# A linear-attention and mixture-of-experts kernel: the state's decay and its copy on VectorE instead of GpSimd

## The chip, the cores and the metric

The kernel runs on one core of a Trainium2 chip. A core has five engines with an instruction stream each: TensorE (PE) multiplies matrices, VectorE (DVE) and GpSimd (POOL) do elementwise work, ScalarE (ACT) copies and applies functions, and SyncE (SP) issues most DMAs. Each takes its own instructions in order; between engines they wait for semaphores. The metric is the device time of one execution in microseconds (us), the median of several runs.

## What is computed

A recurrent attention layer (4 batches, 8 heads, 768 steps, head dimension 40) and behind it a mixture of 8 experts with a normalised gate (3072 tokens of 320 numbers, 1024 hidden):

```python
for t in range(S):
    y[:, :, t] = np.einsum('bhd,bhde->bhe', rt, state)
    Sa = np.einsum('bhde,bhe->bhd', state, at)
    state_decay = state * wt[:, :, None, :] - np.einsum('bhd,bhe->bhde', Sa, bt)
    state = state_decay + np.einsum('bhd,bhe->bhde', vt, kt)
```

```python
logits = x @ w_gate                   # x is y, a row of 320 per token
P = np.exp(logits - logits.max())
for _ in range(8):
    P /= P.sum(1, keepdims=True) + 1e-09
    P /= P.sum(0, keepdims=True) + 1e-09
    P *= N / E
for e in range(E):
    out += P[:, e:e + 1] * (np.maximum(x @ w1[e], 0.0) @ w2[e])
```

Everything is float32.

## The kernel before

**Attention** works in 12 chunks of 64 steps. A step of the kernel is one chunk of one batch, with its 8 heads as 4 pairs (rows 0 to 39 hold one head of a pair, rows 64 to 103 the other); there are 48 such steps. Each has two parts.

`prep(c, b)` (lines 106 to 165) does what does not depend on the state. It loads `inp`, takes running products of the decay along the chunk (`q` at L114, `g` at L122, both scans on DVE), scales keys (`kb`, L133) and the `a` vectors (`ab`, L139 and L140) with them, multiplies the two on PE (`ll`, L145), and transposes `kb` (`kt`, L153). The last column of `q`, the decay over the whole chunk, four numbers per row, is copied into `cc` at L138, since `q` has one buffer and is soon overwritten. `kb` is POOL's in all steps but the first, `ab` from the seventh step on (`NFAST` = 6); before that they are DVE's. For some steps the tiles `cc`, `g`, `sx`, `bb`, `kb` or `inp` lie inside larger raw tiles named `st`, and the trace then shows `st` in their place.

Between the parts stands a block inversion, once per two chunks (`GROUPS`, 6 in all): L170 to L182 on DVE, products of two tensors (`pr`) and reductions, up to 2048 numbers per row, ended by a copy at L331. Its results go to DRAM and back and are put together by PE and ACT (`tload`, `tmat`).

`recur(c, b)` (lines 235 to 302) is the chain through the state: on PE `av` (L251), `xc` (L259), `pu` (L270) and `c2` (L277, `c` in the trace), with the masks `f` (L252) and `pm` (L272) and the sum `ws` (L279) on DVE, and copies on ACT. From `ws` POOL makes the output `y` (L281), and the last 40 columns, the state before decay, are multiplied by the next chunk's `cc` to give `z` (L292). PE transposes `z` (`zt`, L297), ACT copies it into `vz` and `f`, and the next chunk of that batch starts from there. For chunks 0 to 8 `z` is POOL's, for 9 and 10 DVE's; chunk 11 has none.

The four batches run a little apart. Events with times (`ev`, lines 346 to 382) give the order in which the code is written, with up to 17 prepared steps in store (`NSX`). The framework's scheduler then makes each engine's order from its own estimate of when things are ready, so an edit to one instruction can move others.

**The experts** come next (`layer1`, `layer2`). Their first weights and inputs are transformed while attention ends (`prep_w` on POOL and ACT; `prep_x` on DVE and ACT, L517 to L533). From the ninth of 128 blocks on the order is written out by hand (`manual_schedule`); before that it is the scheduler's.

Of the kernel before, what the change touches and what calls it, by code (L numbers as in the profile page):

```python
# [28 lines left out]
def attention(ctx, tc, d, xd, ps, pq, pt, gs, lg):  # L29
    nc = tc.nc  # L30
# [59 lines left out]
    def first_use(i):  # L90
        if i in fresh:
            fresh.discard(i)
            nc.gpsimd.memset(bb_b[i], 0.0)
            nc.scalar.copy(out=sx_b[i][64:R2].rearrange("r p h x -> r (p h) x")[:, :, 64:104],
                           in_=cst[64:R2, 360:400].unsqueeze(1).broadcast_to([40, 8, 40]))
# [3 lines left out]
    def rot(key, lst):  # L99
        i = state[key]  # L100
        state[key] = (i + 1) % len(lst)
        return lst[i]
# [3 lines left out]
    def prep(c, b, ld):  # L106
        cb = c * NB + b
        inp = raws[IN_MAP[cb]][0:R2, 0:1284] if IN_MAP.get(cb) else pin.tile([R2, 1284], F32, name="inp", bufs=2)
        nc.sync.dma_start(out=inp, in_=d["inp"][c, b])
        w65 = inp[:, 0:516]  # L110
        kb_in = inp[:, 516:1028].rearrange("r (p k t) -> r p k t", p=NP, k=2)
        a_in = inp[:, 1028:1284].rearrange("r (p t) -> r p t", p=NP)
        q = pin.tile([R2, NP, 65], F32, name="q")
        nc.vector.tensor_tensor_scan(  # L114
            out=q.rearrange("r p t -> r (p t)"), data0=w65[:, 0:260], data1=one65,
            initial=0.0, op0=ALU.mult, op1=ALU.add)
        g1 = rot("g1", g1_b)
        nc.vector.reciprocal(out=g1[:, :, 0], in_=q[:, :, 64])
        sx = rot("sx", sx_b)
        i = next(j for j in range(NSX) if sx_b[j] is sx)  # L120
        g, bb, cc = g_b[i], bb_b[i], cc_b[i]
        nc.vector.tensor_tensor_scan(  # L122
            out=g.rearrange("r p t -> r (p t)"), data0=w65[:, 260:516],
            data1=g1.rearrange("r p t -> r (p t)"), initial=0.0, op0=ALU.mult, op1=ALU.add)
        if cb < NKB:
            raw = raws[KB_SETS[cb % len(KB_SETS)]]
            kb = raw[0:R2, 0:512].rearrange("r (p k t) -> r p k t", p=NP, k=2)
            lt = raw[0:64, 512:1024].rearrange("r (p k t) -> r p k t", p=NP, k=2)
        else:
            kb = pin.tile([R2, NP, 2, 64], F32, name="kb")  # L130
            lt = pin.tile([64, NP, 2, 64], F32, name="lt")
        eng = nc.vector if cb < NFAST else nc.gpsimd
        (nc.gpsimd if cb in KB_POOL else eng).tensor_tensor(  # L133
            out=kb, in0=kb_in,
            in1=q[:, :, 63::-1].unsqueeze(2).broadcast_to([R2, NP, 2, 64]), op=ALU.mult)
        ab = rot("ab", ab_b)
        first_use(i)
        nc.gpsimd.tensor_copy(out=cc, in_=q[:, :, 64])  # L138
        eng.tensor_tensor(out=ab[0:40, :, 0:64], in0=a_in[0:40], in1=g[0:40], op=ALU.mult)  # L139
        eng.tensor_tensor(out=ab[64:104, :, 64:128], in0=a_in[64:104], in1=g[64:104], op=ALU.mult)  # L140
        nc.scalar.copy(out=sx[64:104, :, 0, 0:64], in_=ab[0:40, :, 0:64])
        nc.scalar.copy(out=sx[64:104, :, 1, 0:64], in_=ab[64:104, :, 64:128])
        ll = pq.tile([128, NP, 2, 64], F32, name="ll", tag="pq")
        for p in range(NP):
            nc.tensor.matmul(ll[:, p], lhsT=kb[:, p], rhs=ab[:, p], start=True, stop=True)  # L145
        if cb < NKB:
            nc.scalar.activation(out=lt, in_=ll[64:128], func=AF.Copy, scale=-1.0)
            (nc.sync if cb < N_SP else nc.scalar).dma_start(out=ld[GRP[c][1], :, b], in_=lt)
            kt = pt.tile([128, NP, 2, 64], F32, name="kt", tag="pt")
        else:  # L150
            kt = pq.tile([128, NP, 2, 64], F32, name="kt", tag="pq")
        for p in range(NP):
            nc.tensor.transpose(kt[:, p].rearrange("s h x -> s (h x)")[:, 0:R2],  # L153
                                kb[:, p].rearrange("r k s -> r (k s)"), ident[0:R2, 0:R2])
        nc.vector.tensor_tensor(
            out=sx[0:64, :, :, 0:64], in0=ll[0:64],
            in1=mask_u.unsqueeze(1).unsqueeze(1).broadcast_to([64, NP, 2, 64]), op=ALU.mult)
        if cb >= NKB:
            nc.scalar.activation(out=lt, in_=ll[64:128], func=AF.Copy, scale=-1.0)
        nc.scalar.copy(out=sx[0:64, :, :, 64:104], in_=kt[0:64, :, :, 0:40])  # L160
        nc.scalar.activation(out=bb[0:64, :, 0:40], in_=kt[64:128, :, 0, 0:40], func=AF.Copy, scale=-1.0)
        nc.scalar.activation(out=bb[64:128, :, 64:104], in_=kt[64:128, :, 1, 0:40], func=AF.Copy, scale=-1.0)
        if cb >= NKB:
            (nc.sync if cb < N_SP else nc.scalar).dma_start(out=ld[GRP[c][1], :, b], in_=lt)
        return dict(cc=cc, g=g, sx=sx, bb=bb)
# [69 lines left out]
    def recur(c, b):  # L235
# [7 lines left out]
                          in_=d["vt"][c, b].rearrange("s (g x) -> s g x", x=40))  # L243
# [6 lines left out]
        for p in range(NP):  # L250
            nc.tensor.matmul(av[:, p], lhsT=vz[:, p], rhs=rb[:, p], start=True, stop=True)  # L251
        nc.vector.tensor_tensor(  # L252
            out=f[:, :, :, 0:64], in0=av,
# [24 lines left out]
        ws = wk.tile([R2, NP, 104], F32, name="ws")  # L278
# [5 lines left out]
        for h in range(2):  # L284
            nc.sync.dma_start(
                out=xd[h * 160:h * 160 + 160].rearrange("(p e) t -> e p t", e=40)[:, :, tok:tok + 64],
                in_=y[h * 64:h * 64 + 40])
        gq.append(gate(c, b, y))
        if c + 1 == NCH:
            return  # L290
        z = wk.tile([R2, NP, 40], F32, name="z", bufs=4)
        (nc.vector if c >= 9 else nc.gpsimd).tensor_tensor(out=z, in0=ws[:, :, 64:104],  # L292
                                in1=preps[c + 1, b]["cc"].unsqueeze(2).broadcast_to([R2, NP, 40]), op=ALU.mult)
        yield
        zt = ps.tile([40, NP, 104], F32, name="zt", tag="ps")
# [52 lines left out]
    def step(c, b):  # L348
        if (c, b) not in gens:
            gens[c, b] = recur(c, b)  # L350
        next(gens[c, b], None)

    def do_prep(s, c, b, first):
        if first:
            start_seg(s)
        preps[c, b] = prep(c, b, invs[s][0])
# [453 lines left out]
```

## Time and profile before

| | us |
|---|---|
| median of 3 runs (lowest, highest) | 1890.27 (1883.09, 1900.79) |
| the profiled execution | 1888.5 |
| its span, first to last instruction | 1886.7 |
| PE busy in the span | 1768.5 |
| DVE busy | 1395.1 |
| POOL busy | 896.9 |
| ACT busy | 853.9 |
| mean granted TensorE clock | 0.945 of full speed |

The span is what the profile's times count in; the rest of the execution's time lies around it. [...] In the lines of the profile `out<-in` gives the tiles that an instruction writes and reads, and `[1.28 <-POOL z L292]` says that the engine sat idle for 1.28 us before it, until the named instruction was done. `un`, `lu`, `pr` and `gt` are the tiles of the inversion.

### The profile page before, as it was taken

How to read it: one execution, taken by the hardware profiler on the slowest of the kernel's cores; microseconds unless marked ns; L12 is line 12 of the kernel's file. 1: busy time of each engine (PE TensorE's matmuls, PEld its weight loads, DVE VectorE, ACT ScalarE, POOL GpSimd, SP SyncE). 2: the span in 40 equal slices, each digit the busy share in tenths (PEclk: the TensorE clock that was granted, in tenths of full speed). 3: DMA queues.
4: the chain of work that ended last, by engine and by line, in shares of the span. 5: the costliest groups of instructions: out<-in, count | busy, mean ns of one | idle time of the engine just before them, and what ended most of it. 6: DMA issues, size and time to landing. Idle time of an engine off the chain costs nothing.

```text
span 1886.7 us, 31821 instructions
## 1 busy us (share of the span) xinstructions
PE 1768.5 (94%) x12035; PEld 1731.1 (92%) x12035; DVE 1395.1 (74%) x2330; ACT 853.9 (45%) x1845; POOL 896.9 (48%) x845
## 2 busy tenths in 40 slices
PE   4478989889998999999999999999999999999999
PEld 4368878789888999999999999999999999999999
DVE  7766768686579877776867777886776767777676
ACT  6346566655553444343433434345343433434342
POOL 6636457562345355371835628004461826537170
PEclk9568889988889999999999999999999999999999
DMA  8567777855732011110201102111110201111011
GB/s 192 102 131 160 137 156 144 176 128 102 164 96 70 32 43 37 37 61 14 73 26 49 55 19 74 55 33 38 37 55 19 73 19 56 37 37 57 17 37 42
DMA packets 187838, 136.26 MB, mean 72 GB/s; under 512 B 155941, under 2 KB 165285, under 8 KB 187685
## 3 DMA queue, kind: packets, MB, share of 16 engines
q1 hardware_dynamic: 184485, 128.98, 27.6%
q10 hardware_dynamic: 3200, 5.25, 1.1%
q8 instruction: 95, 1.56, 0.3%
q14 instruction: 58, 0.48, 0.1%
HBM read 113.74 MB, written 20.45 MB: 71 GB/s over the span
## 4 chain that ended last, share of the span: by engine, by line
PE 76%; DVE 10%; DMA 6%; issue 3%; POOL 2%; ACT 2%; SPq 1%; DVEq 0%; POOLq 0%; ACTq 0%
PE op L610 35%; PE p L545 32%; DMA inp<-in_inp_dram 2%; PE xc L259 2%; DVE pr L179 2%; PE pu L270 1%; PE av L251 1%; PE c L277 1%; DVE q L114 1%; PE ll L145 1%; PE lp L307 1%; PE gp L226 1%; DMA nd<-pr 1%; POOL ab L140 1%; DVE g L122 1%
## 5 line engine op out<-in xcount | busy, mean ns | idle before, releaser
L545 PE MATMUL p<-xch,wh 128*128 128x384 f32 (+1 forms) x1792 | 605.3, 339 | 5.2 <-DVE cs L654 1.8
L566 ACT ACTIVATE hh<-sm 128x384 fp32r<-128x384 f32 x512 | 269.5, 527 | 726.3 <-DVE sm L563 726.3
L610 PE MATMUL op<-wh,hh 128*128 128x320 f32 x1536 | 477.3, 311 | 1.0 <-ACT hh L566 0.9
L610 PE MATMUL op<-wl,hh 128*128 128x320 f32 x1536 | 474.7, 310 | 0.0
L610 PE MATMUL op<-wh,hl 128*128 128x320 f32 x1536 | 468.0, 310 | 4.4 <-DVE hl L569 4.4
L491 POOL TENSOR_TENSOR wl<-ws,wh 128x640 fp32r<-128x640 f32 x60 | 103.1, 1719 | 608.4 <-ACT wh L489 608.1
L569 DVE SCALAR_TENSOR_TENSOR hl<-sm,hh 128x384 fp32r<-128x384 f32 x512 | 370.8, 757 | 2.8 <-ACT hh L566 2.3
L545 PEld LDWEIGHTS p<-xch,wh 128*128 128x128 f32 (+1 forms) x1792 | 337.9, 189 | 8.4 <-DVE u L563 2.7
L545 PE MATMUL p<-xcl,wh 128*128 128x384 f32 x896 | 303.1, 338 | 0.0
L545 PE MATMUL p<-xch,wl 128*128 128x384 f32 x896 | 302.3, 337 | 0.0
L610 PEld LDWEIGHTS op<-wh,hh 128*128 128x128 f32 x1536 | 290.6, 189 | 1.7 <-ACT hh L566 1.5
L610 PEld LDWEIGHTS op<-wh,hl 128*128 128x128 f32 x1536 | 287.1, 188 | 5.4 <-DVE hl L569 5.3
L610 PEld LDWEIGHTS op<-wl,hh 128*128 128x128 f32 x1536 | 291.4, 190 | 0.0
L563 DVE TENSOR_TENSOR sm<-p,u 128x384 f32<-128x384 f32 x384 | 232.6, 615 | 9.2 <-PE p L545 0.4
L545 PEld LDWEIGHTS p<-xcl,wh 128*128 128x128 f32 x896 | 169.0, 189 | 0.0
L545 PEld LDWEIGHTS p<-xch,wl 128*128 128x128 f32 x896 | 169.0, 189 | 0.0
L563 DVE TENSOR_TENSOR sm<-p,p 128x384 f32<-128x384 f32 x128 | 71.3, 557 | 130.1 <-PE p L545 76.2
L563 DVE TENSOR_TENSOR p<-p,p 128x384 f32<-128x384 f32 x128 | 71.1, 555 | 101.5 <-PE p L545 101.0
L563 DVE TENSOR_TENSOR u<-p,p 128x384 f32<-128x384 f32 x128 | 70.8, 553 | 59.4 <-PE p L545 58.1
L145 PE MATMUL ll<-ab,kb 104*128 104x128 f32 x336 | 61.3, 340 | 50.6 <-POOL ab L140 22.2
L499 POOL TENSOR_TENSOR wl<-ss,wh 128x512 fp32r<-128x512 f32 x60 | 90.7, 1512 | 32.1 <-ACT wh L496 28.0
L145 PEld LDWEIGHTS ll<-ab,kb 104*128 104x128 f32 x336 | 53.2, 241 | 54.7 <-POOL ab L140 27.4
(161 smaller groups left out, 2845.0 us busy)
## 6 DMA issues: line engine op xcount, KB each, us to landing
ws<-in_wts_dram SPq DMA_DIRECT2D x60, 832.0 KB
inp<-in_inp_dram SPq DMA_DIRECT2D x42, 521.6 KB
rb<-in_r_dram SPq DMA_DIRECT2D x48, 208.0 KB
ld<-lt ACTq DMA_DIRECT2D x40, 128.0 KB
vz<-in_v_dram SPq DMA_DIRECT2D x48, 104.0 KB
f<-in_vt_dram SPq DMA_DIRECT2D x48, 80.0 KB
xd<-y SPq DMA_DIRECT2D x96, 40.0 KB
st<-in_inp_dram SPq DMA_DIRECT2D x6, 521.6 KB
```

Of the source, the lines that this page charges most:

```text
L114: nc.vector.tensor_tensor_scan(out=q.rearrange("r p t -> r (p t)"), data0=w65[:, 0:260], data1=one65, initial=0.0, op0=ALU.mult, op1=ALU.add)
L122: nc.vector.tensor_tensor_scan(out=g.rearrange("r p t -> r (p t)"), data0=w65[:, 260:516], data1=g1.rearrange("r p t -> r (p t)"), initial ...
L145: nc.tensor.matmul(ll[:, p], lhsT=kb[:, p], rhs=ab[:, p], start=True, stop=True)
L179: nc.vector.tensor_tensor(out=prv, in0=a.unsqueeze(2).broadcast_to([nu, n_c, n_r, n_k]), in1=m.rearrange("u k r -> u r k").unsqueeze(1).br ...
L259: nc.tensor.matmul(xc[h][:, p], lhsT=pp["sx"][:, p, h], rhs=f[:, p, h], start=True, stop=True)
L491: g.tensor_tensor(out=wl[:, 0:640], in0=raw[:, 256:896], in1=wh[:, 0:640], op=ALU.subtract)
L499: g.tensor_tensor(out=lv[:, 3:7], in0=so[:, :, 0], in1=hv[:, 3:7, 0], op=ALU.subtract)
L545: nc.tensor.matmul(o, lhsT=w_, rhs=x_, start=(j == 0), stop=(j == 3))
L563: eng.tensor_tensor(out=out, in0=x, in1=y, op=ALU.add)
L566: nc.scalar.activation(out=hh[:, f, h], in_=sm[f][:, h], func=AF.Relu)
L569: v.scalar_tensor_tensor(out=hl[:, f, h], in0=sm[f][:, h], scalar=0.0, in1=hh[:, f, h], op0=ALU.max, op1=ALU.subtract)
L610: nc.tensor.matmul(ops[i], lhsT=a[:, h, cs], rhs=w_[:, cw], start=(f == 0 and h == 0 and j == 0), stop=(last and h == 1 and j == 2))
```

## The change

Two lines name another engine. `cc` is copied by DVE in all 48 steps, and `z` is DVE's in all chunks, so 48 copies and 36 products of POOL become DVE's. What they compute stays.

```diff
@@ -135,7 +135,7 @@
         first_use(i)
-        nc.gpsimd.tensor_copy(out=cc, in_=q[:, :, 64])
+        nc.vector.tensor_copy(out=cc, in_=q[:, :, 64])
         eng.tensor_tensor(out=ab[0:40, :, 0:64], in0=a_in[0:40], in1=g[0:40], op=ALU.mult)
@@ -289,7 +289,7 @@
         z = wk.tile([R2, NP, 40], F32, name="z", bufs=4)
-        (nc.vector if c >= 9 else nc.gpsimd).tensor_tensor(out=z, in0=ws[:, :, 64:104],
+        nc.vector.tensor_tensor(out=z, in0=ws[:, :, 64:104],
                                 in1=preps[c + 1, b]["cc"].unsqueeze(2).broadcast_to([R2, NP, 40]), op=ALU.mult)
```

The scheduler makes the order of attention anew on every engine. Three places show it. The first is POOL in chunk 0, batches 1 and 2, which are named by the prepared `g` that `y` reads. Before:

```order
L281 TENSOR_TENSOR y<-ws,g_155 104x256
L292 TENSOR_TENSOR z<-ws,cc_172 104x160
L138 COPY cc_160<-q 104x4
L139 TENSOR_TENSOR ab_194<-inp,g_155 40x4x64
L140 TENSOR_TENSOR ab_194<-inp,g_155 40x4x64
L281 TENSOR_TENSOR y<-ws,g_159 104x256
L292 TENSOR_TENSOR z<-ws,cc_176 104x160
L139 TENSOR_TENSOR ab_195<-inp,g_159 40x4x64
L140 TENSOR_TENSOR ab_195<-inp,g_159 40x4x64
L133 TENSOR_TENSOR kb<-inp,q 104x512
```

And with the change:

```order
L281 TENSOR_TENSOR y<-ws,g_155 104x256
L133 TENSOR_TENSOR kb<-inp,q 104x512
L139 TENSOR_TENSOR ab_194<-inp,g_155 40x4x64
L140 TENSOR_TENSOR ab_194<-inp,g_155 40x4x64
L281 TENSOR_TENSOR y<-ws,g_159 104x256
L133 TENSOR_TENSOR kb<-inp,q 104x512
L139 TENSOR_TENSOR ab_195<-inp,g_159 40x4x64
L140 TENSOR_TENSOR ab_195<-inp,g_159 40x4x64
```

`z` and `cc` are gone from POOL, and `kb` stands ahead of `ab` in each step.

The second place is DVE during the second inversion, from the `ws` of chunk 0, batch 3 on. Before:

```order
L279 TENSOR_TENSOR ws<-c_1257,c_203 104x416
L114 SCALAR_TENSOR_TENSOR q<-inp,cst 104x260
L272 TENSOR_TENSOR pm<-pu,cst 128x416
L179 TENSOR_TENSOR pr<-gt,un 128x2048
L118 RECIPROCAL g_196<-q 104x4
L155 TENSOR_TENSOR sx_157<-ll,cst 64x8x64
L182 TENSOR_REDUCE un<-pr 128x16x8
L122 SCALAR_TENSOR_TENSOR g_163<-inp,g_196 104x256
```

With the change:

```order
L279 TENSOR_TENSOR ws<-c_1257,c_203 104x416
L179 TENSOR_TENSOR pr<-gt,un 128x2048
L155 TENSOR_TENSOR sx_157<-ll,cst 64x8x64
L292 TENSOR_TENSOR z<-ws,cc_180 104x160
L122 SCALAR_TENSOR_TENSOR g_163<-inp,g_196 104x256
L272 TENSOR_TENSOR pm<-pu,cst 128x416
L114 SCALAR_TENSOR_TENSOR q<-inp,cst 104x260
L182 TENSOR_REDUCE un<-pr 128x16x8
```

`z` joins behind the product of 2048 numbers and `sx`, while `q` and `pm`, which stood ahead of that product, come behind `z`.

The third place is DVE at the end of attention, from the `ws` of chunk 9, batch 3 on (`xt` belongs to the first input transform of the experts). Before:

```order
L279 TENSOR_TENSOR ws<-c_4960,c_203 104x416
L292 TENSOR_TENSOR z<-ws,st_185 104x160
L312 COPY lg<-lp 64x8 x2
L272 TENSOR_TENSOR pm<-pu,cst 128x416
L252 TENSOR_TENSOR f<-av,cst 104x8x64
L279 TENSOR_TENSOR ws<-c_5043,c_202 104x416
L292 TENSOR_TENSOR z<-ws,st_186 104x160
L272 TENSOR_TENSOR pm<-pu,cst 128x416
```

With the change:

```order
L279 TENSOR_TENSOR ws<-c_4960,c_203 104x416
L292 TENSOR_TENSOR z<-ws,st_185 104x160
L312 COPY lg<-lp 64x8
L272 TENSOR_TENSOR pm<-pu,cst 128x416
L312 COPY lg<-lp 64x8
L252 TENSOR_TENSOR f<-av,cst 104x8x64
L517 TENSOR_TENSOR xt<-xs 128x256
L518 TENSOR_TENSOR xt<-xs 128x256
L521 TENSOR_TENSOR xt<-xs,xt 128x256
L279 TENSOR_TENSOR ws<-c_5043,c_202 104x416
L522 TENSOR_TENSOR xt<-xs,xt 128x256
L292 TENSOR_TENSOR z<-ws,st_186 104x160
```

The first `xt` products, which stood behind the `ws` of chunk 10, batch 1 before, now stand ahead of the `ws` of batch 0.

## The prediction

> **What bounds the kernel now.** I read the page first, for the split of the span, then the busy time by stage, then the lines that the change touches. In the slices a digit is a tenth of busy time, and PEclk is the granted TensorE clock in tenths.
>
> ```profile
> span 1886.7 us, 31821 instructions
> PE 1768.5 (94%) x12035; PEld 1731.1 (92%) x12035; DVE 1395.1 (74%) x2330; ACT 853.9 (45%) x1845; POOL 896.9 (48%) x845
> PE   4478989889998999999999999999999999999999
> DVE  7766768686579877776867777886776767777676
> PEclk9568889988889999999999999999999999999999
> ```
>
> From the twelfth slice on (about 560 us) PE is full at full clock: that is the expert layer, which the change does not touch. The twelve slices before it are attention, where PE shows gaps and a lower clock. By stage (columns: stretch, length, busy time of each engine with its instructions, clock, DMA share, GB/s):
>
> ```profile
> 0.00:56.60 56.60, 28.47 (x152) 25.71 (x152) 39.44 (x68) 32.23 (x78) 34.55 (x58) 0.84 0.83 184
> 56.60:118.80 62.20, 25.27 (x136) 22.96 (x137) 44.42 (x61) 20.35 (x52) 36.85 (x30) 0.50 0.63 118
> 118.80:485.00 366.20, 331.16 (x2942) 309.06 (x2940) 280.80 (x428) 223.78 (x564) 183.12 (x195) 0.88 0.67 138
> 485.00:560.00 75.00, 71.54 (x612) 66.98 (x612) 41.62 (x74) 42.43 (x96) 33.01 (x36) 0.81 0.59 148
> 560.00:1886.70 1326.70, 1312.09 (x8199) 1306.39 (x8198) 988.77 (x1702) 535.13 (x1055) 609.37 (x527) 1.00 0.13 43
> ```
>
> So the most that any attention change can touch is 560 us, and 1% of the whole time is 19 us, 3.4% of attention. In the long third stage PE is busy 331.2 of 366.2 us at 0.88 of full clock, and DVE 280.8. That DVE mean hides two kinds of stretch. I cut the stage at the first and last instruction of each block inversion; the first sum below is over the five stretches that hold one (two are shown), the second over the four between them:
>
> ```profile
> 118.80:163.20 44.40, 39.29 (x367) 36.63 (x366) 43.66 (x63) 26.31 (x66) 26.36 (x23) 0.92 0.56 123
> ...
> 441.70:485.00 43.30, 41.02 (x400) 38.35 (x398) 39.30 (x57) 22.95 (x58) 7.76 (x10) 0.93 0.40 88
> sum 253.40, PE 225.88 PEld 209.91 DVE 233.30 ACT 151.01 POOL 133.07; mean PE 45.18 PEld 41.98 DVE 46.66 ACT 30.20 POOL 26.61
> ...
> sum 112.80, PE 105.28 PEld 99.15 DVE 47.50 ACT 72.77 POOL 50.05; mean PE 26.32 PEld 24.79 DVE 11.87 ACT 18.19 POOL 12.51
> ```
>
> With an inversion DVE is 92% busy (233.3 of 253.4) and leaves 20.1 us; without one it is 42% busy. An instruction added to DVE is therefore free in the second kind and nearly not free in the first.
>
> **The change part by part.** It moves 36 scalings z (chunks 0 to 8; the 8 of chunks 9 and 10 are on DVE already) and 48 copies cc, and adds no arithmetic and no DMA. Their rows (duration min/median/max in ns):
>
> ```profile
> L292 POOL TENSOR_TENSOR z<-ws,cc x20: 445/452/3972, 129.5 to 470.2; 104x160 f32<-104x160 f32 x20
> L292 POOL TENSOR_TENSOR z<-ws,st x16: 444/453/1419, 169.8 to 416.8; 104x160 f32<-104x160 f32 x16
> L292 DVE TENSOR_TENSOR z<-ws,st x5: 324/739/1561, 493.4 to 536.4; 104x160 f32<-104x160 f32 x5
> L292 DVE TENSOR_TENSOR z<-ws,cc x3: 307/319/325, 475.2 to 488.4; 104x160 f32<-104x160 f32 x3
> L138 POOL COPY cc<-q x27: 178/187/3680, 9.9 to 366.6; 104x4 f32<-104x4 f32 x27
> L138 POOL COPY st<-q x21: 180/188/3562, 47.9 to 420.0; 104x4 f32<-104x4 f32 x21
> L118 DVE RECIPROCAL g<-q x48: 157/181/198, 8.2 to 422.0; 104x4 f32<-104x4 f32 x48
> L312 DVE COPY lg<-lp x48: 123/158/160, 143.9 to 561.8; 64x8 f32<-64x8 f32 x48
> ```
>
> *Cost on DVE.* A z has its DVE price in the trace: 0.32 us undisturbed, 0.74 the median of the five that ran beside POOL's weight work. I take 0.32 and keep 0.74 for the range. A 104x4 copy on DVE is not in the trace. The reciprocal reads the same 104x4 numbers in 0.18, a 64x8 copy takes 0.16: I take 0.18, the same shape, and the two are close enough to be both ends. In the changed order 24 of the moved z and 22 of the cc stand inside an inversion's stretch (17 of those cc in the five stretches above, 5 in the first inversion, before 118.8). That is 24 x 0.32 + 22 x 0.18 = 7.7 + 4.0 = 11.7 us where DVE is nearly full. The other 12 z and 26 cc stand where it is idle at least 30% of the time (39.4 of 56.6 us busy at the start, 42% busy between inversions): 8.5 us that I cost at nothing, the cover being those waits. If that cover were gone, they would add their 8.5 us. Of the 11.7 us I let half lengthen the stretches, 5.9: DVE has 20.1 us of waits there, more than is added, but each ends when a PE product or a load arrives, so an instruction fills a wait only when it is ready during one. Nothing and all of it are the ends.
>
> *Gain on POOL.* POOL gets out of 36 x 0.45 + 48 x 0.19 = 25 us of undisturbed work, and POOL is no bound: 183 of 366 us. What counts is lateness. The rows' maxima show it, and a timeline shows where they come from (start, duration, idle before and releaser):
>
> ```profile
> 151.38 0.57 DVE L279 TENSOR_TENSOR ws<-c,c 104x416 f32<-104x416 f32 x1
> 152.97 3.73 DVE L179 TENSOR_TENSOR pr<-gt,un 128x2048 f32<-128x2048 f32 x1
> 153.05 3.97 POOL L292 TENSOR_TENSOR z<-ws,cc 104x160 f32<-104x160 f32 x1
> 157.07 0.54 PE L297 MATMUL zt<-cst,z 104*40 104x104 f32 x4 [1.28 <-POOL z L292]
> ...
> 140.89 0.66 DVE L122 TENSOR_TENSOR_SCAN g<-inp,g 104x256 f32<-104x256 f32 x1
> 141.03 3.02 POOL L138 COPY cc<-q 104x4 f32<-104x4 f32 x1 [2.27 <-DVE q L114]
> 144.01 0.72 POOL L139 TENSOR_TENSOR ab<-inp,g 40x256 f32<-40x256 f32 x1
> 145.59 0.49 PE L145 MATMUL ll<-ab,kb 104*128 104x128 f32 x2 [1.52 <-POOL ab L140]
> ```
>
> A POOL instruction that meets a long DVE product of two SBUF tensors lasts as long as that product: z takes 3.97 us beside a 3.73 us product, not 0.45. A copy of four numbers takes 3.02 us although DVE has finished g, and ab, queued behind it, keeps PE waiting 1.52. [...]
>
> What PE waited for POOL from 120 to 460 us (total, times, longest):
>
> ```profile
> PE ll L145 <- POOL ab L140: 4.5, 4, 1.9
> PE zt L297 <- POOL z L292: 4.4, 3, 2.6
> PE ll L145 <- POOL kb L133: 2.4, 1, 2.4
> ```
>
> The z waits are 4.4 us. But DVE works in order, and the changed order does not put z right behind ws where it hurt. For chunk 0, batch 3 (the 1.28 us wait) there stand the 3.73 us product and the masked copy sx between ws and z, so z ends no sooner than 3.73 + 0.32 = 4.05 us after ws, and later by sx, against 157.02 - 151.95 = 5.1 before. Elsewhere inside inversions one long product or reduction often stands between them too, and pm, the next step's mask, now stands behind such a z or ahead of it by turns. What comes late next at these places is the same zt, released by DVE. I credit half of the 4.4, that is 2.2. The cc copy's own lateness goes, since a copy on DVE is never queued ahead of ab: 1.5. Together 3.7, with 0 and 11.3 (all three rows) as ends.
>
> *Other orders that move.* The start (0 to 118.8) waits for loads and for the chain of preparations; 11 copies join DVE before the first inversion, 2.0 us against 17.2 us of idle time there, and I take nothing. At the end of attention the first input transform of the expert layer moves ahead of chunk 10, batch 0, with its loads. The rows before:
>
> ```profile
> 503.53 0.69 DVE L252 TENSOR_TENSOR f<-av,cst 104x512 f32<-104x512 f32 x1 [3.12 <-PE av L251]
> 517.22 2.76 DVE L517 TENSOR_TENSOR xt<-xs 128x256 f32<-128x256 f32 x1 [1.29 <-DMA xs<-xd]
> ```
>
> In the new order DVE stands at that xt after f, at 504.2. If the load still landed at 517.2 it would wait 13.0 us, with ws and z queued behind; 2.8 us of work would then be done already, so 10.2 at most. The loads move forward in SP's order as well, all five parts in one go but for a small f load, so I take nothing and keep 10.2 as an end.
>
> *Sum.* 5.9 - 3.7 = +2.2 us. The profiled execution took 1888.5 us (span 1886.7 and 1.8 around it), 1.8 below the median of the runs, 1890.27. So 1888.5 + 2.2 = 1890.7, rounded 1891: no change that can be measured.
>
> **The rivals.** *DVE becomes the bound in the inversions (slower).* For it: 92% busy, and z on DVE was 0.74 at the median beside a busy POOL. Then nothing is absorbed and no lateness is gained: 24 x 0.74 + 22 x 0.18 = 21.8, so 1888.5 + 21.8 = 1910.3. It decides from 20.7 us on, where 1% is crossed. Against it: the 20.1 us of waits, and the 0.32 us of the three z at 475 to 488, the first of them within an inversion.
>
> *PE's gaps close and its clock stays up (faster).* The clock falls behind the gaps of 150 to 160 us:
>
> ```profile
> 150.00:160.00 10.00, 6.87 (x73) 6.17 (x73) 10.00 (x10) 5.92 (x17) 7.98 (x6) 1.00 0.80 171
> 160.00:170.00 10.00, 9.95 (x82) 9.76 (x83) 6.57 (x13) 8.44 (x21) 7.37 (x10) 0.83 0.69 171
> 170.00:180.00 10.00, 8.49 (x67) 8.19 (x67) 3.82 (x7) 6.35 (x16) 4.23 (x7) 0.74 0.82 166
> 180.00:190.00 10.00, 10.00 (x68) 8.77 (x67) 4.75 (x9) 6.35 (x16) 2.96 (x5) 0.67 0.96 188
> 190.00:200.00 10.00, 10.00 (x76) 9.58 (x77) 4.14 (x8) 5.13 (x13) 4.21 (x6) 0.73 0.81 143
> ```
>
> The missing clock of 160 to 200 is 10 x (0.17 + 0.26 + 0.33 + 0.27) = 10.3 us. If the three waits above (11.3) and this dip went, and DVE's share were absorbed, the time would be 1888.5 - 21.6 = 1866.9. Against it: z stays late there by the order, and only 1.28 of the 3.13 idle us in 150 to 160 are z's. [...]
>
> *DVE stands at the transform's load (a little slower).* 1890.7 + 10.2 = 1900.9, still within 1%.
>
> *The move does not matter at all*: 1888.5, not to be told from the forecast.
>
> **How the numbers follow.** Forecast, with "does not matter", 0.52; DVE as bound 0.20; gaps and clock 0.15; the load 0.13. One per cent of 1890.27 (18.9 us, about what a measurement of this kernel can tell from no change) puts the bounds at 1871.4 and 1909.2. The whole order of attention is made anew and the clock's dips may fall elsewhere, one dip being worth 10 us by the rows above, so part of the fast case (0.03) stays within 1%, and of the slow one 0.18 lies beyond, the rest within. Faster 0.12, same 0.70, slower 0.18. The range takes in the load's case whole, reaches up to 1911 for the DVE case at its price, and down to 1871 to where the fast case leaves 1%: about 0.12 lies below and 0.08 above.
>
> **What would show it.** Right: DVE's busy time to 485 us up by some 20 us, POOL's down by at least 25, L292 all on DVE with a median near 0.32, the waits of PE on z turned into waits on a DVE z, the end of attention within a few us of 560. The copies on DVE must be near 0.18. The DVE rival shows as longer inversion stretches, above 44.4 and 43.3 us in the first and last; the clock rival as 0.9 or more from 160 to 200; the load as a wait of xt on xs of more than 1.3 us. The prediction is wrong if attention ends 20 us away from 560 in either direction, or if the expert layer's 1326.7 us change.

## The result, and the profile after

| | before | after |
|---|---|---|
| median of 4 runs each, on one chip (us) | 1886.68 | 1919.07 |
| lowest and highest | 1882.89, 1900.79 | 1918.14, 1922.95 |
| ratio, with its 95% interval | | 1.0157 [1.0116, 1.0198] |

The change made the kernel slower, by 32 us or 1.6%. The forecast was 1891, with a range to 1911. Ratios, here and below, are estimated from the single runs of both kernels, leaving out the few slow ones, and are not quite those of the medians. The page of the changed kernel (an execution of 1919.1 us):

```profile
span 1917.3 us, 31788 instructions
PE 1792.3 (93%) x12035; PEld 1752.8 (91%) x12035; DVE 1414.4 (74%) x2414; ACT 854.2 (45%) x1845; POOL 866.8 (45%) x761
PEclk8558778988868999999999999999999999999999
```

DVE does 19.3 us more and POOL 30.1 less, as forecast. PE is 23.8 us longer busy with the same 12035 products, and in its clock row a 5, two 7s and a 6 stand where a 6 and three 8s stood. The moved instructions in the changed kernel (duration min/median/max in ns):

```profile
L292 DVE TENSOR_TENSOR z<-ws,cc x23: 302/325/941, 132.5 to 503.8; 104x160 f32<-104x160 f32 x23
L292 DVE TENSOR_TENSOR z<-ws,st x21: 298/325/1552, 180.6 to 562.6; 104x160 f32<-104x160 f32 x21
L138 DVE COPY cc<-q x27: 131/159/1153, 8.9 to 384.0; 104x4 f32<-104x4 f32 x27
L138 DVE COPY st<-q x21: 130/170/1056, 50.2 to 441.7; 104x4 f32<-104x4 f32 x21
```

The prices were right too: 0.325 us for `z` (0.32 taken), 0.16 to 0.17 for the copy (0.18 taken). Where the time went shows when attention is cut at the recurrence itself, at the `ws` of chunk 3, chunk 9, chunk 10 and chunk 11 (batch 3 each). Columns as in the table by stage: stretch, length, busy time of PE, PEld, DVE, ACT and POOL, clock, DMA share, GB/s. Before:

```profile
118.80:267.00 148.20, 133.55 (x1169) 124.70 (x1167) 116.73 (x177) 92.54 (x233) 81.48 (x87) 0.88 0.69 141
267.00:493.40 226.40, 206.00 (x1847) 192.29 (x1846) 167.82 (x259) 135.67 (x344) 102.51 (x109) 0.88 0.67 138
493.40:534.80 41.40, 37.94 (x328) 35.28 (x327) 23.41 (x38) 26.85 (x59) 22.30 (x22) 0.78 0.77 197
534.80:559.20 24.40, 24.40 (x212) 22.96 (x212) 13.89 (x28) 11.15 (x25) 9.12 (x13) 0.89 0.22 58
559.20:1886.70 1327.50, 1312.89 (x8204) 1307.19 (x8202) 989.33 (x1703) 535.13 (x1055) 610.10 (x527) 1.00 0.13 43
```

And after:

```profile
118.80:290.10 171.30, 152.71 (x1223) 143.14 (x1222) 129.31 (x211) 97.16 (x245) 76.77 (x60) 0.78 0.67 138
290.10:508.00 217.90, 195.77 (x1784) 182.75 (x1784) 175.65 (x290) 132.15 (x334) 84.42 (x71) 0.90 0.63 133
508.00:562.50 54.50, 50.78 (x326) 46.63 (x326) 27.83 (x46) 27.78 (x61) 29.76 (x29) 0.60 0.66 170
562.50:592.70 30.20, 30.20 (x229) 28.05 (x229) 8.86 (x21) 10.13 (x23) 3.73 (x5) 0.76 0.06 13
592.70:1917.30 1324.60, 1311.89 (x8200) 1306.00 (x8198) 987.66 (x1703) 535.31 (x1055) 610.08 (x527) 1.00 0.13 43
```

Chunks 0 to 3 take 23.1 us more and 4 to 9 8.5 less; the two belong together, since 54 products more stand in the first and 63 fewer in the second. Up to the `ws` of chunk 9 that is +14.6 us. Chunk 10 takes 13.1 us more, chunk 11 5.8 more, and the experts 2.9 less: 30.6 in all, the difference of the spans. The second inversion starts at 118.8 and 119.2 us, so the start has hardly a share in it.

Two things can lengthen a stretch in which PE has the same work: idle time (length less busy time) and lost clock (busy time times one less the clock). At a lower clock the same products took longer: in the changed kernel the eight `av` of a step took 1.04 us at 505.1 us, where the granted clock was 1.00, and 2.04 us at 521.2 us, where it was 0.50. In chunk 10 idle time is 3.5 us before and 3.7 after; lost clock is 37.94 x 0.22 = 8.3 before and 50.78 x 0.40 = 20.3 after. In the same way chunk 11 loses 2.7 and 7.2, and chunks 0 to 9 lose 16.0 + 24.7 = 40.7 and 33.6 + 19.6 = 53.2. The sum over attention is +29.0 us of lost clock and +5.9 of idle time, against +33.5 of length. The slower kernel hardly waits more; its PE runs at a lower clock (0.60 in chunk 10, where it was 0.78). What is to be found is why.

### The profile page after: what moved, and what is told of

Its sections match the earlier page's. It is cut to its first block, busy times and chain, and to the rows that moved or that the text cites. A ratio compares the mean times of both kernels' runs of the same rounds, so it can differ in the third digit from the quotient of the medians.

```text
span 1917.3 us, 31788 instructions
## 1 busy us (share of the span) xinstructions
PE 1792.3 (93%) x12035; PEld 1752.8 (91%) x12035; DVE 1414.4 (74%) x2414; ACT 854.2 (45%) x1845; POOL 866.8 (45%) x761
## 4 chain that ended last, share of the span: by engine, by line
PE 75%; DVE 10%; DMA 5%; issue 2%; POOL 1%; ACT 1%; SPq 1%; DVEq 0%; ACTq 0%; POOLq 0%
PE op L610 34%; PE p L545 32%; DMA inp<-in_inp_dram 3%; PE xc L259 2%; DVE pr L179 2%; PE pu L270 1%; PE av L251 1%; PE c L277 1%; DVE hl L569 1%; PE lp L307 1%; PE ll L145 1%; PE gp L226 1%; DVE q L114 1%; DVE sm L563 1%; PE op L231 1%
## 5 line engine op out<-in xcount | busy, mean ns | idle before, releaser
L545 PEld LDWEIGHTS p<-xch,wh 128*128 128x128 f32 (+1 forms) x1792 | 338.1, 189 | 10.5 <-DVE sm L563 4.8
```

Of the source, the lines that this page charges most:

```text
L545: nc.tensor.matmul(o, lhsT=w_, rhs=x_, start=(j == 0), stop=(j == 3))
```

## The experiments

**Engine or order?** The change does two things: 84 instructions run on another engine, and the scheduler makes every engine's order anew. To part them, the order of a kernel was recorded and imposed on another one, by edges that fix the order of issue within an engine and add no wait:

```diff
+def pin(tc):
...
+    here = {i.name: i for i in tc.nc.cur_bb.bb.instructions}
+    for text in SEQ:
...
+            tc.add_manual_dep(ins, prev.name, mybir.DependencyInfo(
+                mybir.DependencyClass.NoSync, mybir.DependencyReason.DATA), reason="pin")
+            prev = ins
```

`SEQ` holds the recorded order, one text for each engine. Each half alone was run this way, and each moved line alone with the scheduler's own order (`copy_only` changes L138, `scale_only` L292).

> z and cc are VectorE's in all steps, as in the changed kernel, but every engine issues in the order of the kernel before; z stands directly behind its ws and cc directly behind the reciprocal of its step. The changed kernel stood 32 us above the one before (1919 against 1887). Theory A (VectorE's added work, 84 instructions of 20 us in all, is the cost): about 1919, at least 1907. Theory B (the order that the scheduler made anew is the cost): 1880 to 1892. If both count, between.

> The counterpart: z and cc are GpSimd's as in the kernel before, but all other instructions of every engine stand in the order of the changed kernel; on GpSimd z stands behind its y, cc ahead of the kb and ab of its step. Theory A (VectorE's added work): 1882 to 1895, the time before. Theory B (the new order): about 1919, at least 1907. Above 1919 would say that VectorE's version of z and cc is the better one in that order.

> Only cc moves to VectorE, z stays; the scheduler makes its own order. Theory A, in proportion to VectorE's time (48 x 0.18 = 8.6 of 20.2 us): 1887 + 0.43 x 32 = 1901. Theory B: the time has nothing to do with that share; anything from 1875 to 1920, and it need not add up with the run that moves z alone.

> Only z moves to VectorE, cc stays; the scheduler makes its own order. Theory A, in proportion to VectorE's time (36 x 0.32 = 11.5 of 20.2 us): 1887 + 0.57 x 32 = 1905, and with the copy's run the two excesses make up the whole 32. Theory B: anything from 1875 to 1920, not in proportion, and the two excesses do not add up.

| z and cc on | order of the rest | median | ratio to before |
|---|---|---|---|
| DVE | before | 1894.77 | 1.0032 [1.0009, 1.0055] |
| POOL | after | 1922.61 | 1.0167 [1.0128, 1.0206] |
| cc on DVE, z on POOL | the scheduler's | 1893.78 | 1.0030 [1.0005, 1.0055] |
| z on DVE, cc on POOL | the scheduler's | 1907.48 | 1.0100 [1.0067, 1.0133] |

The new order with the old engines has the whole loss; the new engines in the old order cost 6 us by the ratio, and their 1894.77 lies 3 us above what theory B had for them. Theory B holds for nearly all of the loss. The edges themselves cost nothing that shows: the kernel before with its own order fixed by them, less 48 small products, took 1886.10 (`thin_old` below). The rows of the old order with the new engines, cut at the same `ws` of chunks 3, 9 and 10:

```profile
118.80:275.70 156.90, 139.67 (x1170) 130.32 (x1169) 125.77 (x209) 94.12 (x237) 63.92 (x60) 0.83 0.67 136
275.70:500.60 224.90, 200.35 (x1836) 187.49 (x1836) 181.58 (x295) 135.69 (x344) 82.75 (x72) 0.90 0.68 139
500.60:541.40 40.80, 37.62 (x345) 35.25 (x346) 20.06 (x39) 26.02 (x58) 19.98 (x21) 0.83 0.83 204
```

And of the new order with the old engines:

```profile
118.80:282.60 163.80, 148.65 (x1212) 138.67 (x1213) 120.79 (x180) 96.57 (x244) 85.99 (x90) 0.81 0.70 141
282.60:508.10 225.50, 198.52 (x1790) 185.31 (x1789) 167.86 (x255) 132.19 (x335) 100.40 (x108) 0.87 0.61 130
508.10:564.20 56.10, 51.96 (x326) 47.95 (x327) 27.74 (x47) 27.88 (x61) 29.97 (x29) 0.58 0.64 167
```

Chunk 10 takes 54.5 and 56.1 us in the new order, whatever the engines, 41.4 and 40.8 in the old. Up to the `ws` of chunk 9 the engines count too: 374.6 us before, 381.8 with the new engines, 389.3 with the new order, 389.2 with both. The run with `z` alone lost at another place, in chunks 4 to 9 (261.8 us at a clock of 0.76, in an execution 15 us above its median), and nothing in chunk 10 (37.9). Its time is also near what theory A had for it (1905), so it is the place that speaks against A. A loss that moves about with each new order is no price of an instruction.

**Which part of the order?** The orders were joined at the `ws` of chunk 9, batch 3: all that one order issues up to it, then the rest in the other.

> z and cc on VectorE. All engines in the order of the kernel before up to the ws of chunk 9, batch 3 (about 500 us), from there in the order of the changed kernel. In the two runs that have the new order throughout, the stretch from that ws to the end of attention took 85 and 86 us, in the one with the old order 62. Theory B1 (the order at the end makes the loss there): 1895 + 22 = 1917, with the expert layer's start inside the gap about 1910 to 1920. Theory B2 (the end is only late because what comes before it is late and out of step): about 1895, at most 1902.

> The counterpart: z and cc on VectorE, the new order up to the ws of chunk 9, batch 3, from there the order of the kernel before. Theory B1: 1919 - 22 = 1897, at most 1904; the stretch behind that ws about 62 us. Theory B2: about 1919, at least 1912, the stretch about 85 us.

Old, then new: 1909.39, ratio 1.0119 [1.0050, 1.0188], chunk 10 in 54.9 us. New, then old: 1906.15, 1.0104 [1.0049, 1.0160], chunk 10 in 44.8 us. Neither theory has all of it. By the ratios the end costs 0.87% (1.0119 less 1.0032) or 0.53% (1.0157 less 1.0104), 10 to 16 us, and the order ahead of it 0.38% or 0.72%, 7 to 14 us; the intervals are as wide as that.

**What lets the clock fall at the end?** Up to 510.0 us PE of the changed kernel waits 2.73 us for a load, and the clock falls behind it (1.00 from 508 to 512 us, 0.53 from 512 to 516). Ten-us rows of the changed kernel:

```profile
506.00:516.00 10.00, 6.43 (x61) 6.09 (x60) 1.77 (x4) 3.59 (x10) 0.73 (x1) 0.81 0.72 139
516.00:526.00 10.00, 10.00 (x57) 8.79 (x57) 1.44 (x3) 2.77 (x7) 2.81 (x4) 0.50 0.89 269
526.00:536.00 10.00, 10.00 (x70) 9.05 (x70) 4.05 (x9) 5.95 (x12) 4.56 (x5) 0.67 0.62 129
536.00:546.00 10.00, 10.00 (x62) 9.73 (x62) 9.00 (x12) 6.86 (x16) 9.69 (x7) 0.50 0.52 165
```

From 516 to 546 us PE is busy all the time at 0.50 to 0.67 of full clock. The first idea was to fill the gap:

```diff
         gp = pt.tile([64, 2 * NP, 32], F32, name="gp", tag="pt")
+        for _ in range(FILL.get((c, half), 0)):
+            nc.tensor.matmul(gp.rearrange("a p x -> a (p x)"), lhsT=cst[:, 0:64], rhs=cst[:, 400:656],
+                             start=True, stop=True)
...
+FILL = {(10, 0): 7}
```

> The changed kernel in its own order, with 7 products of constants (128x64 by 128x256) added on TensorE right ahead of the first gp of chunk 10, where it waited 2.7 us for td at 510 us; their results are overwritten by gp. They put work into a gap and take none out. Theory C (the loss at the end is TensorE's clock, which that gap lets fall, and which then stays near half for 50 us): the clock from 512 to 564 us stays above 0.8 and 10 to 20 us go, 1899 to 1909. Theory C' (the clock falls for other reasons, or the loss is in the order of the work and not in the clock): no gain, 1917 to 1923.

1920.08, ratio 1.0171 [1.0108, 1.0233]: nothing gained. The rows are of the fastest of its four runs (1910.63 to 1931.81 us). All but 0.8 us of the gap was filled, and the clock fell a few us later all the same:

```profile
506.00:516.00 10.00, 8.41 (x80) 6.82 (x78) 2.06 (x4) 4.58 (x12) 0.54 (x1) 1.00 0.77 171
516.00:526.00 10.00, 9.74 (x56) 8.51 (x55) 1.32 (x4) 2.72 (x6) 2.09 (x3) 0.56 0.80 237
```

So it is not the gap alone. What PE does from there on is seen in the timeline of the changed kernel (start, duration, and behind the tiles the columns moved, the last number):

```profile
516.28 0.90 PE L259 MATMUL xc<-f,sx 104*104 104x104 f32 x4
517.11 0.38 PE L307 MATMUL lp<-gs,y 104*64 104x8 f32 x2
517.42 1.02 PE L259 MATMUL xc<-f,sx 104*104 104x104 f32 x4
```

The gate's products `lp`, which move 8 columns, stand between the pairs of `xc`. In the old order (here with the new engines) they stand in blocks there, and `xc` runs in one piece. The clock falls there too (0.50 from 506 to 510 us; the `pu` at 506.4 us takes 2.04 us, as in the changed kernel), but it is back from 510 us on (1.00 from 510 to 514). At 510.5 `av` takes 1.04 us and not the 2.04 that it takes at 521.2 us in the changed kernel:

```profile
505.45 0.99 PE L307 MATMUL lp<-gs,y 104*64 104x8 f32 x8 [0.34 <-DVE lg L312]
...
508.21 2.48 PE L259 MATMUL xc<-f,sx 104*104 104x104 f32 x16
510.52 1.04 PE L251 MATMUL av<-rb,vz 104*104 104x128 f32 x8
```

From 516.7 us on that order has `xc` and `lp` in turn as well, but by then at full clock (0.61 and 0.28 us for the forms that take 1.02 and 0.38 above), and there the clock stays at 1.00 until 522 us (0.71 from 522 to 526).

Does PE's clock depend on what it is busy with? A kernel with nothing but streams of such products was to tell, and the changed kernel with three quarters of the late `lp` left out, beside the same in the kernel before:

```diff
         for p in range(NP):
-            nc.tensor.matmul(lp, lhsT=y[:, p], rhs=gs[:, p], start=(p == 0), stop=(p == NP - 1))
+            if c < THIN or p == NP - 1:
+                nc.tensor.matmul(lp, lhsT=y[:, p], rhs=gs[:, p], start=(c >= THIN or p == 0), stop=(p == NP - 1))
...
+THIN = 8
```

> Nothing of the reference is computed; zeros are returned. TensorE alone runs streams of the forms that attention is made of, each once from a pause of about 13 us and once behind 16 wide products (128x512): products with 104 columns (as in xc), two of these and one with 8 columns in turn (as xc and lp stand at the end of attention), 8 columns alone (lp), 32 columns alone (gp), and groups of four 104-column products with a wait for VectorE between them. Theory C2 (products that keep the engine busy but move few columns count as little work, and the clock falls or stays low under them): clock near 1.0 for 104 columns alone, 0.5 for 8 and for 32 columns alone and for the mixture, also behind the wide products. Theory C1 (only idle time counts, and a TensorE that is busy for some us gets full clock): 1.0 in all four streams some us after their start, 0.5 only with the waits.

> The changed kernel in its own order, leaving out three of the four gate products (lp, 8 columns each) in each step of chunks 8 to 11, 48 in all, so that the gate's logits of these tokens are not the reference's. The 48 are 16 x 3/4 x 0.63 = 7.6 us of TensorE's work at full clock, about 10 at the clock there. Theory C2 (the thin products between those of xc hold the clock down at the end): the clock lost in chunks 10 and 11 (29 us of the changed kernel) falls below 12, and the time to 1890 to 1897. Theory C1: only the work goes, 1909 to 1913, with some 25 us of lost clock left there.

> The same 48 products left out of the kernel before, in its own order (the logits of the same tokens are not the reference's): the control. Both theories: 1890 less the work, 1879 to 1886, with 5 to 11 us of lost clock in chunks 10 and 11. The difference between this run and the one in the changed order is what remains of the 32 us: by theory C2 at most 14, by theory C1 at least 24.

Rows of the streams kernel (PE, PEld, DVE and POOL busy, clock): 104 columns alone from the start, where the clock stood at 1.0; the mixture (one 8-column product behind every two of 104) from a pause, and the same behind wide products, early and late; 8 columns alone from a pause; 32 columns alone from a pause:

```profile
25.00:45.00 20.00, 20.00 (x207) 20.00 (x207) 0.00 (x0) 0.00 (x0) 1.00 0.01 2
...
110.00:160.00 50.00, 50.00 (x239) 41.67 (x237) 0.00 (x0) 0.00 (x0) 0.50 0.00 1
190.00:200.00 10.00, 10.00 (x82) 8.32 (x81) 0.00 (x0) 0.00 (x0) 1.00 0.00 0
205.00:230.00 25.00, 25.00 (x121) 20.91 (x120) 0.00 (x0) 0.00 (x0) 0.50 0.00 1
245.00:270.00 25.00, 25.00 (x237) 25.00 (x236) 0.00 (x0) 0.00 (x0) 0.50 0.01 1
...
335.00:365.00 30.00, 30.00 (x284) 30.00 (x283) 0.00 (x0) 0.00 (x0) 0.50 0.01 1
```

PE is busy without a break in each row, and its clock is 1.0 in some and 0.5 in others: theory C2, not C1. C2 had the mixture at 0.5 behind wide products too; there it held 1.0 for some 16 us first. (The pauses were of 8.2 us, where the expectations say 13. Four 104-column products with a wait for DVE behind them, busy 28.9 of 35 us, also stayed at 0.5.) In the kernel itself, chunks 10 and 11 of the changed order with those `lp` left out:

```profile
512.40:563.50 51.10, 38.87 (x295) 35.79 (x295) 28.92 (x46) 27.81 (x61) 27.45 (x26) 0.73 0.69 177
563.50:585.00 21.50, 20.67 (x188) 19.21 (x188) 11.39 (x20) 10.15 (x23) 5.92 (x9) 1.00 0.13 30
```

The lost clock falls from 20.3 and 7.2 us to 10.5 and 0, as C2 says. But the time was 1912.46, ratio 1.0140 [1.0085, 1.0194], and the control 1886.10, 0.9995 [0.9971, 1.0018]: 26 us apart, which C1 had. Chunk 11 is down to 21.5 us; in chunk 10 idle time rose from 3.7 to 12.2. The two chunks took 72.6 us, 12.1 less than with all `lp`; the control, with the same products left out, saved 6.0 there. With the clock back, something else was late. The trace of this run shows what: DVE waits 6.63 us at an input transform of the experts, PE waits for the `ws` behind it, and then for an `x` that stands behind nine transforms on ScalarE:

```profile
532.14 0.42 DVE L519 TENSOR_TENSOR xt<-xs 128x256 f32<-128x256 f32 x1 [6.63 <-DMA xs<-xd]
...
533.78 2.04 PE L251 MATMUL av<-rb,vz 104*104 104x128 f32 x8 [2.97 <-DVE ws L279]
...
544.18 2.04 PE L270 MATMUL pu<-x,tt 128*128 128x104 f32 x8 [3.87 <-ACT x L265]
```

These two waits are 6.8 of the 12.2 us. In the changed kernel PE, at its lower clock (0.60 over chunk 10, 0.73 in this run), is still busy at these places: its 3.7 us hold no wait for `ws` or `x`.

**What else is late at the end?** The experts' first transforms. The edit regroups the recorded orders: attention's instructions in one kernel's order, the experts' behind as many of attention's on each engine as in the other.

> z and cc on VectorE. Attention's instructions stand in the changed kernel's order on every engine, but those of the experts' first transforms (loads of xs and ws, xt, xch, xcl, wh, wl, ss, and the first products) stand where the kernel before has them: behind as many of attention's instructions on the same engine. On VectorE the first xt then has 26 instead of 35 of attention's instructions behind it, on ScalarE the first nine copies 45 to 33 instead of 48 to 44. Theory D (the early transforms, queued ahead of the recurrence of chunk 10 on VectorE and ScalarE, make the loss of the end): 1919 less 10 to 16, 1903 to 1909, as with the old order behind chunk 9 (1906). Theory D' (the order of attention's own work at the end makes it): 1915 to 1923.

> The counterpart: attention in the order of the kernel before (z and cc on VectorE), the experts' first transforms at the places that they have in the changed kernel. Theory D: 1895 plus 10 to 16, 1905 to 1911, as with the whole new order behind chunk 9 (1909). Theory D': 1893 to 1898.

Old attention with the early transforms: 1912.30, ratio 1.0121 [1.0084, 1.0158], against 1.0032 without: 0.89%, 17 us. DVE stands at the first `xt` until its load lands, `ws` behind it, and PE's next `av` waits 3.04 us for that `ws`; ScalarE takes nine transforms in a row, 5.5 us, ahead of `x`. DVE's timeline in that run (an execution 8 us below its median):

```profile
523.37 0.42 DVE L517 TENSOR_TENSOR xt<-xs 128x256 f32<-128x256 f32 x1 [7.41 <-DMA xs<-xd]
...
524.39 0.58 DVE L279 TENSOR_TENSOR ws<-c,c 104x416 f32<-104x416 f32 x1
```

And ScalarE's:

```profile
526.83 0.83 ACT L485 CAST wh<-ws 128x768 fp32r<-128x768 f32 x1
...
532.36 0.49 ACT L265 COPY x<-xc 64x416 f32<-64x416 f32 x1
```

The counterpart gave nothing back: 1919.23, 1.0142 [1.0094, 1.0190], against 1.0157. Chunk 10 took 51.8 us with the early transforms alone and 51.9 with the new attention order alone, 54.5 with both. Of these, idle time and lost clock are 9.2 and 12.8 us with the early transforms alone, 4.1 and 14.3 with the attention order alone (in an execution 11 us below its median), 3.7 and 20.3 with both, and 3.5 and 8.3 before. Theory D is right one way and not the other: either is enough for most of the loss of chunk 10, so they do not add up, and taking one away frees little. The thinned run shows how: waits for the transforms and PE's slow stretch lie side by side, and where the one goes, the other is left.

**Which engine's order ahead of the end, and would later transforms help the kernel before?** Single engines' orders were exchanged in the joined kernel (new, then old end), and the transforms moved back in the kernel before.

> As the run with the new order up to chunk 9 and the old one behind it (1906; 166 us from 118.8 us to the ws of chunk 3, batch 3), but VectorE has the old order throughout, z directly behind its ws. Theory E (the place of the recurrence's masks, sums and z between the long products of the inversion on VectorE makes the loss of chunks 0 to 3): about 157 us there and 1895 in all, at most 1900. Theory E' (another engine's order): 163 us or more, 1902 to 1910.

> The same with GpSimd in the old order too. If GpSimd's kb, which stands ahead of ab in the new order, is what is late: 1895 here and 1906 with VectorE alone in the old order, 157 us against 166 from 118.8 us to the ws of chunk 3, batch 3. If VectorE's order is the cause both are 1895, if neither is, both 1906.

> The run with the new order up to chunk 9 and the old one behind it (1906), with SyncE alone in the old order. Theory F (loads of rb, v and td are issued late in the new order; the changed kernel waited 2.3 us for rb at 195 us and for td at 280 us): 1895 to 1900 and 157 to 160 us from 118.8 us to the ws of chunk 3, batch 3. Otherwise 1903 to 1910.

> The kernel before, with z and cc on GpSimd and its own order, but the experts' first transforms and their loads stand a quarter later (the first xt with 19 instead of 26 of attention's instructions behind it on VectorE, ScalarE's first copies with 33 instead of 44) and their first products behind nearly all of attention's on TensorE. Theory D (early transforms delay the recurrence at the end): chunk 10 takes less than its 41 us, and the time is 1880 to 1887, unless the expert layer then waits for its inputs. If the old place costs nothing: 1888 to 1895.

VectorE old: 1944.04, 1.0273 [1.0227, 1.0319]. VectorE and GpSimd old: 1944.13, 1.0268. Both are outside what either theory said. Half of what VectorE's old order adds to the joined kernel lies in chunks 4 to 9 (247.2 us against 228.2). The likely reading, which no row shows, is that an engine with an order that the others don't have is out of step with them. So this does not tell which queue makes the loss ahead of the end. The stretch by which the expectations judge was badly chosen as well, since the orders put different products into chunks 0 to 3. SyncE old: 1909.85, 1.0111 [1.0076, 1.0147], theory F is out. Later transforms in the kernel before: 1918.05, 1.0140 [1.0097, 1.0184], also outside both: chunk 10 was no faster (42.5), and now ScalarE's and DVE's transforms stood in front of chunk 11, which took 49.3 us instead of 24.4.

**From which mixture on does the clock stay down?** Two more kernels of streams alone.

> Nothing of the reference is computed; zeros are returned. As in the first run of streams, each stream once behind a pause of about 13 us with the clock at 0.5 and once behind 16 wide products: 104 columns alone, 104 columns with one 8-column product behind every eighth and behind every fourth, 64 columns alone, 128 columns alone. In the first run 104 columns alone held 1.0 but were not started at 0.5, and the mixture with one 8-column product behind every second held 1.0 for 15 us and never rose from 0.5. If the share of time in which columns move decides, 128 and 104 columns alone rise from 0.5 within some 10 us, 64 columns stay at 0.5, and of the mixtures the one with every eighth rises and the one with every fourth is at the edge. If 104 columns alone stay at 0.5 too, attention has no product that brings the clock back, and only the start of wide ones or chance does.

> Nothing of the reference is computed; zeros are returned. Streams of products with 104, 112 and 120 columns alone, each from a pause of about 13 us with the clock at 0.5 and once behind 16 wide products (64 columns first, to set the start). In the run before 128 columns alone rose from 0.5 within 5 us, and 104 columns with one 8-column product behind every eighth stayed at 0.5 for 40 us. If the edge lies between 104 and 128 columns, 104 stays at 0.5 and one of the others rises, and the products of the recurrence other than av can hold a full clock but not bring it back. If 104 rises, it was the 8-column products alone that kept the clock down.

Rows of the first: 104 columns with an 8-column product behind every eighth, from a pause and behind wide products; 64 columns alone, likewise; 128 columns alone from a pause.

```profile
110.00:150.00 40.00, 40.00 (x217) 37.50 (x217) 0.00 (x0) 0.00 (x0) 0.50 0.00 1
175.00:195.00 20.00, 20.00 (x196) 18.67 (x196) 0.00 (x0) 0.00 (x0) 1.00 0.01 2
...
310.00:355.00 45.00, 45.00 (x262) 45.00 (x261) 0.00 (x0) 0.00 (x0) 0.50 0.00 1
385.00:405.00 20.00, 20.00 (x221) 20.00 (x220) 0.00 (x0) 0.00 (x0) 1.00 0.01 2
416.00:421.00 5.00, 5.00 (x23) 5.00 (x24) 0.00 (x0) 0.00 (x0) 0.50 0.00 0
421.00:426.00 5.00, 5.00 (x44) 5.00 (x43) 0.00 (x0) 0.00 (x0) 0.92 0.02 3
```

Rows of the second, 104 columns alone from a pause:

```profile
96.40:101.40 5.00, 5.00 (x29) 5.00 (x30) 0.00 (x0) 0.00 (x0) 0.50 0.00 2
101.40:106.40 5.00, 5.00 (x49) 5.00 (x49) 0.00 (x0) 0.00 (x0) 0.85 0.01 3
106.40:126.00 19.60, 19.60 (x217) 19.60 (x216) 0.00 (x0) 0.00 (x0) 1.00 0.00 1
```

104 columns alone bring the clock back within 10 us. One 8-column product behind every eighth of them, which was expected to let it rise, keeps it at 0.5 for 40 us, though the same mixture holds 1.0 once it is there; so does one behind every fourth (0.50 from 210 to 250 us, 1.00 from 275 to 300). In the changed order one `lp` stands behind every two `xc`. Whether the kernel gains when each gate's four `lp` are issued in one block was not tried.

## Why the prediction was wrong

- *Cost on DVE, and gain on POOL: 5.9 - 3.7 = +2.2.* The prices and the busy times were right, and the sum was near: alone, in the old order, the new engines cost 0.32% [0.09, 0.55], 2 to 10 us. The gain depends on the order: PE's waits for `z`, 4.4 us before, are 1.4 with the new engines in the old order and 8.6 in the changed kernel.
- *Other orders that move: "I take nothing" for the start, and nothing for the end with 10.2 as its bound.* **This is the step that failed.** For the start, taking nothing was about right (118.8 and 119.2 us to the second inversion). But the order itself cost 1.67% [1.28, 2.06], all of the loss. Ahead of the end it was examined only for where `z` stands, and at the end only for DVE's `xt`, not for ScalarE's transforms nor for PE's `lp`. Attention ended at 592.7 us, 33 away from 560, where the prediction had put 20 as a sign of being wrong.
- *The loads move forward in SP's order, so I take nothing.* They did not land in time: `xt` waited 3.77 us in the changed kernel, 7.41 with the early transforms alone. The early transforms cost 17 us there (0.89%), more than the bound of 10.2; that counted DVE's wait alone, not ScalarE's queue nor the clock.
- *The clock.* The forecast priced a dip at 10 us and let dips fall where they may, which kept 0.03 of the fast chance and 0.02 of the slow one within 1%. The lost clock grew by 29.0 us, nearly the whole loss. One dip's price was about right (chunk 10 lost 12.0 more); that the new order could have several more was not.
- *The rivals.* The inversions' first and last stretch took 57.9 and 42.5 us against 44.4 and 43.3. In the first DVE is busy 48.2 of the 57.9 us, so it is not what bounds it. With the new engines in the old order it is busy 47.8 of 48.6: there the DVE rival does show, by 4 us, and that run's 0.32% rules it out as the main cause. (Of the five `z` with the median of 0.74, four ran beside POOL's weight work; the sum 24 x 0.74 + 22 x 0.18 gives 21.7 and not 21.8.) POOL's `y` took 0.73 us at the median before and after; eight of the eleven that took over 1 us in the changed kernel, the one of 4.15 us at 164.5 us among them, ran beside a product of the inversion on DVE (there one of 3.78 us). The transform's load was the one with its sign in the trace, but it was held within 1%, and no case had it together with the clock.
- *The range* ended at 1911 because each case was added to the forecast alone. The load's bound (10.2) and one more dip (10) together would have given 1911 as a middle, not as an end.
- *The clock falls behind gaps.* In the changed kernel no gap of the end exceeds 2.8 us; the clock fell behind one of 2.73 us and was 0.50 to 0.67 from 516 to 546 us without any. The streams were busy for 40 and 50 us at 0.50. In these runs the clock went with what PE was busy with, not with how long it was busy.
- *Ahead of the end* the order costs 7 to 14 us by the ratios. That it is the order is shown; which queue, and whether the same thin products let the clock fall there, is not.

## What to carry to other kernels

When a scheduler makes the order, a change of one line is two changes, and the second has to be priced from the order itself: every engine's queue wherever work of two stages meets, not only the queues that the diff names. Pinning the old order onto the new code tells the two apart in one run. Where an engine's clock changes along the run (PE's lay between 0.50 and 1.00 here), count lost clock (busy time times one less the clock) beside idle time, stage by stage: a slower kernel may hardly wait more (here +5.9 us, beside +29.0 of lost clock). And do not take an off-stage transform as free because its engine has time: in that engine's order it stands in front of the recurrence, and too early and too late both cost 17 us and more here.

## What was not expected of the hardware

All of this was measured on the three kernels of streams above, one execution of each. In streams of products that kept TensorE busy without an idle moment, its granted clock followed which products they were, not how long it was busy. Streams of 104, 112, 120 and 128 columns alone rose from 0.50 to 1.00 within some 10 us. Streams of 64, 32 or 8 columns, and 104 columns with one 8-column product in three, five or nine, stayed at 0.50 for the 32 to 57 us that they ran. The clock that a stream started with counted too: behind wide products, at 1.00, the 64 columns and the mixtures with one in five or nine held 1.00 for the 20 us and more that they ran; with one 8-column product in three the clock fell after some 16 us, with 8 or 32 columns alone after some 5. What it is in the products was not shown: at 1.00 the streams of 64 and of 104 columns alone had 58 records in 5 us each, so the number of columns and the columns per us change together in them.
